# A batch's last half block computed in the fourth block's tile, with full-size products, k casts on GpSimd and later expert work

## The chip, the cores and the metric

The kernel runs on one core of a Trainium2 chip. The metric is the device time of one execution in microseconds (us); lower is better. The core has five engines that run their own instruction queues side by side: TensorE (PE, matrix products; PEld is its loading of weights), VectorE (DVE), ScalarE (ACT), GpSimd (POOL) and SyncE (SP, which here only issues DMAs). They meet through semaphores.

## The reference

Two stages, the output of the first being the input of the second.

Attention: q, k and v of 8 batches, 8 heads, 576 positions, 64 columns. A position sees itself and the 127 before it (`rel >= 0` and `rel < 128`), with a bias of minus slope times distance, one slope a head. Softmax, then the product with v. This gives x, 4608 tokens by 512 columns.

Mixture of experts: `logits = x @ w_gate` (8 experts), an exponential, eight rounds of dividing rows and columns by their sums (Sinkhorn), and then

```
for e in range(E):
    h = np.maximum(x @ w1[e], 0.0)
    ye = h @ w2[e]
    out += P[:, e:e + 1] * ye
```

with 1024 hidden columns an expert. So all eight experts run on all tokens.

## The kernel before

**The two halves of the span.** Until about 279 us the attention runs, with experts 0 and 1 of blocks that are ready as filler on PE. Then comes Sinkhorn, with the rest of that filler, and from about 332 us the experts 2 to 7, mostly in a seven-product (Strassen) form. The change touches the first half.

**Blocks and steps.** A batch of 576 positions is four blocks of 128 (kb = 0 to 3) and a last half block of 64 (kb = 4, `TL` = 64). The main loop (line 693) runs over steps (b, kb, u), u being one half of the heads; `at = 2 * kb + u` counts the ten steps of a batch. A step first prepares the next one: `scores` (key block kb against query blocks kb and kb + 1, PE, lines 407 to 428), `exps` (ACT, line 434), `masks` (DVE, a product with a table of the decayed and masked weights, line 447). Between them the filler issues expert matmuls. Then `values` of the present step (PE, line 472): queries of block kb against keys of block kb - 1 and kb; the 65th column of v is one, so the sum of the weights comes along. DVE divides (lines 482 and 483), and `turn_x` brings the result into the transposed form for the experts: by PE in batches 0 to 2 and 7, by a transposing DMA on SP in batches 3 to 6.

**The half block.** Its queries and keys lie in a tile of their own, tT: queries in columns 0 to 63, keys in columns 64 to 127. The scores of kb = 3 are 192 wide (128 own queries and 64 of the half block), those of kb = 4 are 64 by 64 with 64 keys. The values of kb = 4 use 64 columns of weights: four products with 128 keys and four with 64.

**How q and k get there.** `load_qk(b + 2)` is issued in batch b at step 3 (SP, line 275). `cast_qk` brings them to half precision, q on DVE and k on ACT, in four parts: from batch 4 on, two parts at steps 8 and 9 of batch b and two at steps 0 and 1 of batch b + 1. Then `turn_qk` transposes them by DMA (SP, line 305) and `order_qk` puts the rows in order: k on GpSimd right away, q on DVE at steps 6 and 7 (line 316). The scores of the next batch are issued in step 9. Batches 0 to 2 use PE transposes instead (`turn_pe`).

**The order of the work.** Each engine executes its instructions in the order in which the program issues them; nothing is reordered. A cast that waits for a load therefore holds all that was issued behind it on the same engine.

**The filler.** `Filler` holds units of expert work (blocks of tokens, expert 0 or 1). `filler.ready` says up to which block x exists. In each step the backlog is divided by `left`, the number of steps it is to be spread over (line 696), and that much is issued. For batches over `XPE` = 3 a batch's blocks become ready after step 0 of the next one (line 742).

**GpSimd** casts v five blocks ahead (`cast_v`, lines 388 and 389, with a memset of the column of ones), casts some parts of q and the half blocks, and issues the loads of the experts' weights.

**Constant matmuls.** `spin` and `spin_alone` issue matmuls on a constant tile (line 253) whose result nobody reads.

Of the kernel before, what the change touches and what calls it, by code (L numbers as in the profile page):

```python
# [14 lines left out]
def kernel(  # L15
# [10 lines left out]
    nc = tc.nc  # L26
# [206 lines left out]
    if True:  # L233
        mask = asb.tile([P, H, 2 * P], FP16, name="mask")
        rel = per.tile([P, HD], FP16, name="rel", tag="yo", bufs=YO)[:, 0 : 2 * P]

        def make_mask(ys):
            for y in ys:
                nc.scalar.activation(
                    out=mask[:, y, :], in_=rel, func=AF.Exp, scale=-float(slopes[head_of[y]])  # L240
                )

# [78 lines left out]
        def turn_tail(b):  # L321
            t16 = asb.tile([P, HD], FP16, name=f"t16_{b}", tag="xsb", bufs=XSB)
            nc.gpsimd.tensor_copy(out=t16, in_=tails.pop(b).rearrange("p h d -> p (h d)"))
            nc.sync.dma_start(out=QKT[b][2], in_=t16, transpose=True)
# [21 lines left out]
        def turn_pe(b, kq, j):  # L346
# [16 lines left out]
            if wide:  # L363
                nc.scalar.copy(out=QKT[b][2], in_=ps)
                return
# [18 lines left out]
        def cast_v(m):  # L384
# [4 lines left out]
            nc.gpsimd.memset(vt[:, :, Dh : Dh + 2], 1.0)  # L389
# [8 lines left out]
        def sizes(kb):  # L398
            nk = P if kb < NKB - 1 else TL
            nn = 0 if kb == NKB - 1 else (P if kb < NKB - 2 else TL)  # L400
            return nk, nn
# [5 lines left out]
        def scores(b, kb, u):  # L407

            nk, nn = sizes(kb)
            ps = sps.tile([P, 2, 2, 2 * P], FP32, name=f"psS_{b}_{kb}_{u}", tag="psS", bufs=2)  # L410
            both = kb < NKB - 2
            for y in range(2):
                j = 2 * u + y
                for hb in range(2):
                    n = 2 * P if both else nk
                    nc.tensor.matmul(  # L416
                        out=ps[0:nk, hb, y, 0:n],
                        lhsT=cols(b, 1, j, hb, kb),
                        rhs=cols(b, 0, j, hb, kb, 1 + both),
                    )  # L420
                for hb in range(2):
                    if nn and not both:
                        nc.tensor.matmul(
                            out=ps[0:nk, hb, y, nk : nk + nn],
                            lhsT=cols(b, 1, j, hb, kb),
                            rhs=cols(b, 0, j, hb, kb + 1),
                        )
            pss[b, kb, u] = ps

        def exps(b, kb, u):  # L430
            nk, nn = sizes(kb)
            ps = pss.pop((b, kb, u))
            pt = asb.tile([P, 4, 2 * P], FP16, name=f"pt_{b}_{kb}_{u}", tag="pt", bufs=4)
            nc.scalar.activation(  # L434
                out=pt[0:nk, :, 0 : nk + nn],
                in_=ps[0:nk, :, :, 0 : nk + nn].rearrange("p a y n -> p (a y) n"),
                func=AF.Exp,
                scale=scale,
            )
            pts[b, kb, u] = pt  # L440

        def masks(b, kb, u):
            nk, nn = sizes(kb)
            pt = pts[b, kb, u]
            hs = slice(4 * u, 4 * u + 4)
            w = nk + nn
# [802 lines left out]
```

## Time and profile before

| | us |
|---|---|
| median of three runs | 1013.42 |
| lowest and highest run | 1010.76, 1014.03 |
| the profiled execution | 1012.89 |
| its span, first to last instruction | 1011.1 |
| PE busy | 998.0 |
| DVE busy | 758.4 |
| ACT busy | 727.4 |
| POOL busy | 79.2 |

A row of instructions in order of time has its start, its length, engine, line, operation, output and inputs by the program's names, and in brackets the idle time before it with what ended it. `128*64` behind a matmul is the size of its weights (rows by columns), the shape after it that of the output. Lengths of neighbouring PE instructions overlap, so what a group costs is read from its start to the start of the next. In a row of a group, the busy time and the mean of one instruction stand behind the bar. `SPq` is the issue of a DMA; when it lands is not in that row.

### The profile page before, as it was taken

To read this page: it belongs to the slowest core of one execution; us is meant where nothing else is said; L and a number is where in the kernel's file an instruction comes from. 1 tells how busy PE (TensorE), PEld (TensorE's weight loads), DVE (VectorE), ACT (ScalarE), POOL (GpSimd) and SP (SyncE) were. 2 spreads that over 40 slices of the span, in tenths; PEclk is the share of its full clock that TensorE was granted. 3 is DMA by queue.
4 is the path that set the end of the run, shared out by engine and by line. 5 is a ranking of instruction groups with operands and counts; after the bars stand their busy time and mean duration, and the time that the engine had idled before them with its cause. 6 is when DMAs were issued, how large, how long until landed. Compare 5 with 4: busy or idle time off the path is not lost.

```text
span 1011.1 us, 27987 instructions
## 1 busy us (share of the span) xinstructions
PE 998.0 (99%) x11583; PEld 802.8 (79%) x11583; DVE 758.4 (75%) x1614; ACT 727.4 (72%) x1252; POOL 79.2 (8%) x143
## 2 busy tenths in 40 slices
PE   8999999999999999999999999999999999999998
PEld 5645444444544799999999999999999999999997
DVE  5737666655578989877877887887887787787787
ACT  7655554555333668888888888888888888888885
POOL 2312033315110000000000000000000000000000
PEclk9999999999999999999999999999999999999999
DMA  9997689888999334334333324335433333433361
GB/s 239 232 268 190 153 224 227 190 191 162 225 192 195 75 64 98 77 65 96 74 65 95 74 65 97 80 62 99 82 66 88 86 80 69 96 75 69 96 116 48
DMA packets 264431, 122.46 MB, mean 121 GB/s; under 512 B 201968, under 2 KB 255728, under 8 KB 264304
## 3 DMA queue, kind: packets, MB, share of 16 engines
q1 hardware_dynamic: 249568, 102.68, 44.8%
q0 software_dynamic: 14304, 17.84, 10.5%
q8 instruction: 90, 1.47, 0.6%
q14 instruction: 37, 0.30, 0.1%
q10 hardware_dynamic: 432, 0.16, 0.1%
HBM read 78.30 MB, written 23.59 MB: 101 GB/s over the span
## 4 chain that ended last, share of the span: by engine, by line
PE 92%; DVE 3%; DMA 2%; ACT 1%; issue 0%; SPq 0%; POOL 0%; DVEq 0%; ACTq 0%; POOLq 0%
PE psM L1020 31%; PE psB L983 14%; PE psh L117 12%; PE psy L141 11%; PE psA L983 9%; PE psC L983 9%; PE psN L472 2%; DMA k<-in_k_dram 2%; PE psS L416 2%; ACT pt L434 1%; PE psT L355 1%; PE psX L510 0%; DMA qk<-c 0%; DVE pt L447 0%; PE psh L962 0%
## 5 line engine op out<-in xcount | busy, mean ns | idle before, releaser
L1020 PEld LDWEIGHTS <-hs 128*128 128x128 f16 x2996 | 270.9, 98 | 22.6 <-DVE hs L1000 0.4
L1020 PE MATMUL psM<-w2l,hs 128*128 128x256 f16 x1440 | 186.7, 273 | 0.2 <-DVE hs L1000 0.2
L983 PEld LDWEIGHTS <-w1l 128*128 128x128 f16 x2848 | 181.3, 98 | 4.9 <-issue 0.5
L996 ACT ACTIVATE hs<-hs 128x512 f16<-128x512 f16 x212 | 130.2, 629 | 35.4 <-DVE hs L1166 25.8
L983 PEld LDWEIGHTS <-s 128*128 128x128 f16 x2136 | 141.6, 98 | 6.5
L1166 DVE TENSOR_TENSOR hs<-psB,s5y 128x512 f16<-128x512 f32 x106 | 73.3, 691 | 97.6 <-ACT xs L892 89.4
L117 PE MATMUL psh<-xT,w1t 128*128 128x512 f16 (+1 forms) x608 | 140.1, 372 | 0.4 <-ACT hT L129 0.4
L892 ACT ACTIVATE xs<-xtok,L_sb 128x512 f16<-128x512 f16 x204 | 136.3, 721 | 3.8 <-DMA xset<-xs 3.6
L129 ACT ACTIVATE hT<-psh 128x512 f16<-128x512 f32 (+1 forms) x144 | 83.3, 586 | 75.9 <-PE psh L117 75.8
L141 PE MATMUL psy<-w2t,hT 128*128 128x512 f16 x576 | 135.5, 380 | 0.0
L1020 PE MATMUL psM<-more,hs 128*128 128x256 f16 x864 | 129.5, 273 | 0.0
L983 PE MATMUL psB<-xset,s 128*128 128x128 f16 x1424 | 108.7, 219 | 0.0
L983 PE MATMUL psA<-xset,w1l 128*128 128x128 f16 x1424 | 108.6, 219 | 0.0
L141 PEld LDWEIGHTS <-hT 128*128 128x128 f16 x576 | 53.4, 98 | 59.6 <-issue 1.9
L434 ACT ACTIVATE pt<-psS 128x1024 f16<-128x1024 f32 (+2 forms) x80 | 67.6, 851 | 43.7 <-PE psS L416 20.3
L117 PEld LDWEIGHTS <-w1t 128*128 128x128 f16 x608 | 55.1, 99 | 53.3 <-issue 4.3
L559 DVE CAST yo<-psy 128x512 f16<-128x512 f32 x65 | 44.7, 691 | 61.6 <-PE psy L141 59.1
L1000 DVE TENSOR_TENSOR hs<-hs 128x1024 f16<-128x1024 f16 x107 | 73.9, 690 | 20.9 <-ACT hs L996 18.8
L1157 ACT COPY psC<-psB 128x512 f32<-128x512 f32 x106 | 60.4, 570 | 39.1 <-PE psB L983 39.1
L1149 ACT COPY s5y<-psC 128x512 f32<-128x512 f32 x106 | 62.1, 586 | 21.6 <-PE psC L983 21.5
L447 DVE TENSOR_TENSOR pt<-pt,mask 128x1024 f16<-128x1024 f16 (+2 forms) x80 | 52.4, 656 | 33.5 <-ACT pt L434 33.4
L1064 DVE TENSOR_TENSOR acc<-acc,psM 128x256 f32<-128x256 f32 (+1 forms) x162 | 73.9, 502 | 0.3
(122 smaller groups left out, 1400.1 us busy)
## 6 DMA issues: line engine op xcount, KB each, us to landing
s5y<-ysp SPq DMA_DIRECT2D x36, 256.0 KB, 3.0
ysp<-yo SPq DMA_DIRECT2D x65, 128.0 KB, 3.5
v<-in_v_dram SPq DMA_DIRECT2D x32, 256.0 KB, 4.2
out_dram<-acc SPq DMA_DIRECT2D x31, 256.0 KB, 2.5
q<-in_q_dram SPq DMA_DIRECT2D x5, 1024.0 KB, 7.7
k<-in_k_dram SPq DMA_DIRECT2D x5, 1024.0 KB, 9.4
xtok<-xd SPq DMA_DIRECT2D x34, 128.0 KB, 2.2
w2t<-in_moe_w_dram POOLq DMA_DIRECT2D x4, 1024.0 KB, 12.6
```

Source lines behind the costliest of these rows:

```text
L117: nc.tensor.matmul(out=ps[:, 0:nt], lhsT=w1ts[e][:, dt, P * ft : P * ft + P], rhs=xT[:, at : at + nb, dt, :], start=(dt == 0), stop=(dt == ...
L129: nc.scalar.activation(out=st["hT"][:, ft, 0:nt], in_=ps[:, 0:nt], func=AF.Relu)
L141: nc.tensor.matmul(out=ps, lhsT=st["hT"][:, ft, P * ms : P * ms + P], rhs=w2ts[e][:, ft, :], start=(ft == 0), stop=(ft == NFT - 1),)
L434: nc.scalar.activation(out=pt[0:nk, :, 0 : nk + nn], in_=ps[0:nk, :, :, 0 : nk + nn].rearrange("p a y n -> p (a y) n"), func=AF.Exp, scale ...
L892: nc.scalar.mul(out=xs[2 * (n % 2) + m], in_=xtok[m], mul=P_sb[:, blk, e : e + 1])
L983: nc.tensor.matmul(out=ps[:, j, :], lhsT=q[k][:, P * j : P * j + P], rhs=xset[n % 2][:, x, P * k : P * k + P], start=(start and j == 0 and ...
L996: nc.scalar.activation(out=h[n][:, slot], in_=src, func=AF.Relu)
L1000: nc.vector.tensor_tensor(out=t[:, 4:6], in0=t[:, 0:2], in1=t[:, 2:4], op=ALU.add)
L1020: nc.tensor.matmul(out=Ms[bk][:, half, :], lhsT=h[n][:, LEFT[m], f, :], rhs=W2L[e][RIGHT[m]][:, f, :], start=(e == 2 and f == 0 and half = ...
L1064: nc.vector.tensor_tensor(out=a, in0=a, in1=p2, op=op)
L1149: nc.scalar.copy(out=s5, in_=pc)
L1166: nc.vector.tensor_tensor(out=h[n][:, 3], in0=pb, in1=s5, op=ALU.add)
```

## The change

1. `scores` of kb = 4 are dropped as a step. The tile of kb = 3 becomes 256 wide: columns 0 to 63 are the half block's keys against its queries, 64 to 127 the fourth block's keys against the half block's queries, 128 to 255 the fourth block against itself. tT gets 64 zero columns, so that the half block's 64 keys are loaded as 128 columns of weights.
2. `exps` and `masks` of kb = 4 go; those of kb = 3 work on 1024 columns instead of 768. The mask table is 3 x 128 wide, its first part made on GpSimd in `tail_masks`.
3. `values` always uses 128 columns of weights and 128 rows; for the half block the lower 64 rows of v are set to zero, its ones included.
4. k's cast is on GpSimd from batch 3 on.
5. The filler's units of a batch become ready after step 1 of the next batch, and `left` is moved by one step (and by one for batch 3).
6. Eight constant matmuls stand ahead of the values of step (1, 1, 0).
7. At the start, two v casts, two q casts and the load of expert 0's w2 stand later in the program, behind `tail_masks`.

```diff
-        mask = asb.tile([P, H, 2 * P], FP16, name="mask")
+        mask = asb.tile([P, H, 3 * P], FP16, name="mask")
+        mask_of = {kb: mask[:, :, P : 3 * P] if kb < NKB - 2 else mask[:, :, 0 : 2 * P] for kb in range(NKB - 1)}
...
+        def tail_masks():
+
+            nc.gpsimd.memset(mask[TL:P, :, 0:TL], 0.0)
+            nc.gpsimd.tensor_copy(out=mask[0:TL, :, 0:TL], in_=mask[0:TL, :, P : P + TL])
+            nc.gpsimd.tensor_copy(out=mask[:, :, TL:P], in_=mask[:, :, 2 * P : 2 * P + TL])
...
-            TT = asb.tile([P, NDT, P], FP16, name=f"tT_{b}", tag="tT", bufs=2)
+            TT = asb.tile([P, NDT, P + TL], FP16, name=f"tT_{b}", tag="tT", bufs=2)
+            nc.gpsimd.memset(TT[:, :, P : P + TL], 0.0)
...
-            nc.gpsimd.memset(vt[:, :, Dh : Dh + 2], 1.0)
+            if nk < P:
+                nc.gpsimd.memset(vt[nk:P], 0.0)
+            nc.gpsimd.memset(vt[0:nk, :, Dh : Dh + 2], 1.0)
...
             for y in range(2):
                 j = 2 * u + y
-                for hb in range(2):
-                    n = 2 * P if both else nk
-                    nc.tensor.matmul(
-                        out=ps[0:nk, hb, y, 0:n],
-                        lhsT=cols(b, 1, j, hb, kb),
-                        rhs=cols(b, 0, j, hb, kb, 1 + both),
-                    )
-                for hb in range(2):
-                    if nn and not both:
-                        nc.tensor.matmul(
-                            out=ps[0:nk, hb, y, nk : nk + nn],
-                            lhsT=cols(b, 1, j, hb, kb),
-                            rhs=cols(b, 0, j, hb, kb + 1),
-                        )
+                if kb < NKB - 2:
+                    parts = [(0, 2 * P, [cols(b, 1, j, hb, kb) for hb in range(2)], [cols(b, 0, j, hb, kb, 2) for hb in range(2)])]
+                else:
+                    tail_q = [cols(b, 0, j, hb, NKB - 1) for hb in range(2)]
+                    tail_k = [QKT[b][2][64 * hb : 64 * hb + 64, j, TL : TL + P] for hb in range(2)]
+                    own_k = [cols(b, 1, j, hb, kb) for hb in range(2)]
+                    parts = [
+                        (P, P, own_k, [cols(b, 0, j, hb, kb) for hb in range(2)]),
+                        (TL, TL, own_k, tail_q),
+                        (0, TL, tail_k, tail_q),
+                    ]
+                for at, n, ks, qs in parts:
+                    for hb in range(2):
+                        nc.tensor.matmul(out=ps[:, hb, y, at : at + n], lhsT=ks[hb], rhs=qs[hb])
...
-                        ops.append((hh, pts[b, kb - 1, u][:, 2 * hb + y, P : P + nk], vs[b, kb - 1][:, 4 * u + hh, 0 : Dh + 1]))
-                    ops.append((hh, pts[b, kb, u][0:nk, 2 * hb + y, 0:nk], vs[b, kb][0:nk, 4 * u + hh, 0 : Dh + 1]))
-            if kb == NKB - 1:
-                ops = ops[0::2] + ops[1::2]
+                        t, at = (pts[b, kb - 1, u], P) if kb < NKB - 1 else (pts[b, kb - 1, u], TL)
+                        ops.append((hh, t[:, 2 * hb + y, at : at + P], vs[b, kb - 1][:, 4 * u + hh, 0 : Dh + 1]))
+                    t, at = (pts[b, kb, u], P * (kb == NKB - 2)) if kb < NKB - 1 else (pts[b, kb - 1, u], 0)
+                    ops.append((hh, t[:, 2 * hb + y, at : at + P], vs[b, kb][:, 4 * u + hh, 0 : Dh + 1]))
...
-        cast_v(3)
-        cast_v(4)
-        for j in (2, 3):
-            cast_qk(1, j, (0,), True)
-        load_weights(0, 1, 2)
...
             turn_pe(0, 1, j)
             turn_pe(0, 0, j)
+        tail_masks()
+        cast_v(3)
+        cast_v(4)
+        for j in (2, 3):
+            cast_qk(1, j, (0,), True)
+        load_weights(0, 1, 2)
...
-            left = ((10 - at) % 10 + 1) if b >= XPE else 10 - at + 9 * (at == 9)
-            budget = filler.backlog() / (11 if (b, at) == (XPE, 0) else left)
+            left = (11 - at) % 10 + 1 if b > XPE else 12 - at if b == XPE else 10 - at + 9 * (at == 9)
+            budget = filler.backlog() / left
...
-                elif nxt[2] == 0:
+                elif nxt[2] == 0 and nxt[1] < NKB - 1:
                     scores(*nxt)
                     scores(*nxt[:2], 1)
-                exps(*nxt)
+                if nxt[1] < NKB - 1:
+                    exps(*nxt)
             got = filler.fill(1.0) if b else 0.0
-            if nxt:
+            if nxt and nxt[1] < NKB - 1:
                 masks(*nxt)
+            if (b, kb, u) == (1, 1, 0):
+                spin_alone(8)
             values(b, kb, u)
...
-            if at == 0 and b > XPE:
+            if at == 1 and b > XPE:
                 filler.ready = 4 * b
...
             if XPE <= b + 1 < B - 1 and at >= 8:
-                cast_qk(b + 2, at - 8)
+                cast_qk(b + 2, at - 8, (1,), True)
+                cast_qk(b + 2, at - 8, (0,))
             if XPE <= b + 1 < B:
                 if at == 0 and b + 1 == XPE:
-                    cast_qk(b + 1, 0)
-                    cast_qk(b + 1, 1)
+                    for j in range(2):
+                        cast_qk(b + 1, j, (1,), True)
+                        cast_qk(b + 1, j, (0,))
                 if at < 2:
-                    cast_qk(b + 1, at + 2)
+                    cast_qk(b + 1, at + 2, (1,), True)
+                    cast_qk(b + 1, at + 2, (0,))
```

More of the change, by code (lines that the diff above doesn't have):

```diff
@@ L239, in make_mask @@
                 nc.scalar.activation(
-                    out=mask[:, y, :], in_=rel, func=AF.Exp, scale=-float(slopes[head_of[y]])
+                    out=mask[:, y, P : 3 * P], in_=rel, func=AF.Exp, scale=-float(slopes[head_of[y]])
                 )
+        def tail_masks():
+            nc.gpsimd.memset(mask[TL:P, :, 0:TL], 0.0)
+            nc.gpsimd.tensor_copy(out=mask[0:TL, :, 0:TL], in_=mask[0:TL, :, P : P + TL])
+            nc.gpsimd.tensor_copy(out=mask[:, :, TL:P], in_=mask[:, :, 2 * P : 2 * P + TL])
         raw: dict = {}
@@ L440, in exps @@
             pts[b, kb, u] = pt
         def masks(b, kb, u):
-            nk, nn = sizes(kb)
             pt = pts[b, kb, u]
-            hs = slice(4 * u, 4 * u + 4)
-            w = nk + nn
-            nc.vector.tensor_tensor(
-                out=pt[0:nk, :, 0:w], in0=pt[0:nk, :, 0:w], in1=mask[0:nk, hs, 0:w], op=ALU.mult
-            )
+            nc.vector.tensor_tensor(out=pt, in0=pt, in1=mask_of[kb][:, 4 * u : 4 * u + 4, :], op=ALU.mult)
         xsbs: dict = {}
         def values(b, kb, u):
-            nk, _ = sizes(kb)
+            nk = sizes(kb)
```

22 lines of the change are left out of this document (6 added, 16 removed).

## The prediction

> **What bounds the kernel now.** I read the page's busy times first, then the list of waits of PE, then the busy times by stage around the one dip of the clock, and last the instructions in order of time there and in one undisturbed batch. Page, part 1, then the one row of PE's waits that is over 1.1 us in total, then four stages (columns: stretch, its length, busy us and count of PE, weight loads, DVE, ACT, POOL, granted clock, DMA share, GB/s):
>
> ```profile
> PE 998.0 (99%) x11583; PEld 802.8 (79%) x11583; DVE 758.4 (75%) x1614; ACT 727.4 (72%) x1252; POOL 79.2 (8%) x143
> ```
> ```profile
> PE psN L472 <- DVE pt L447: 4.6, 6, 1.7
> ```
> ```profile
> 25.00:50.00 25.00, 23.44 (x285) 16.91 (x283) 19.34 (x49) 16.36 (x29) 7.66 (x17) 1.00 1.11 233
> 139.80:141.50 1.70, 0.01 (x1) 0.00 (x0) 0.71 (x2) 1.70 (x4) 0.13 (x1) 1.00 1.25 271
> 141.50:144.00 2.50, 2.38 (x19) 1.10 (x20) 2.43 (x7) 2.12 (x3) 0.53 (x2) 0.80 0.51 134
> 144.00:147.80 3.80, 3.80 (x17) 1.55 (x16) 1.91 (x6) 1.83 (x4) 0.66 (x2) 0.68 0.58 168
> ```
>
> PE is busy 99% of the span, so time can be gained in two ways only: fewer or quicker matmuls, and fewer waits of PE. PE's waits on the mask product (L447) are 4.6 us in all, one of them 1.7. That one lies at 139.8 us, where PE stands still for 1.70 us, and behind it the granted clock is 0.80 for 2.5 us and 0.68 for 3.8 us: 0.20 x 2.5 + 0.32 x 3.8 = 1.7 us more are lost to the clock. The first row is for comparison: 1.56 us idle in several pieces, clock 1.00.
>
> Who holds PE at 139.8, in order of time on PE, ACT, DVE and SP:
>
> ```profile
> 135.05 0.61 PE L416 MATMUL psS<-qN,kN 64*128 64x256 f16 x8
> ...
> 137.91 1.90 PE L141 MATMUL psy<-w2t,hT 128*128 128x512 f16 x8
> 141.54 0.30 PE L472 MATMUL psN<-v,pt 128*128 128x65 f16 x4 [1.73 <-DVE pt L447]
> ```
> ```profile
> 139.22 0.62 ACT L293 CAST c<-k 128x512 f16<-128x512 f32 x1 [7.39 <-DMA k<-in_k_dram]
> 139.74 1.02 ACT L434 ACTIVATE pt<-psS 128x1024 f16<-128x1024 f32 x1
> ```
> ```profile
> 133.55 1.14 DVE L316 COPY qN<-qk 128x512 f16<-128x512 f16 x2
> ...
> 136.28 0.43 DVE L291 CAST c<-q 128x512 f16<-128x512 f32 x1
> ...
> 140.79 0.69 DVE L447 TENSOR_TENSOR pt<-pt,mask 128x1024 f16<-128x1024 f16 x1 [2.57 <-ACT pt L434]
> ```
> ```profile
> 128.54 2.28 SPq L275 DMA_DIRECT2D q<-in_q_dram  x1
> 130.87 0.58 SPq L275 DMA_DIRECT2D k<-in_k_dram  x1
> ```
>
> The scores were ready at about 135.6, but ACT sat 7.39 us in front of a k cast whose load was issued only at 130.87. The exponential stood behind that cast in ACT's queue, the mask product behind the exponential, and PE behind the mask product. This is the step from batch 3 to batch 4; the cast is of batch 5.
>
> **The change part by part.** *The values of a last half block* (`values`, kb = 4) are 8 matmuls per step, 4 with 128x64 and 4 with 64x64 weights; the change makes all 8 full 128x128, at the same 65 columns. One undisturbed batch on PE:
>
> ```profile
> 192.18 0.19 PE L423 MATMUL psS<-tT,kN 64*128 64x64 f16 x2
> 192.20 0.22 PE L416 MATMUL psS<-qN,kN 64*128 64x128 f16 x2
> ...
> 194.53 1.89 PE L141 MATMUL psy<-w2t,hT 128*128 128x512 f16 x8
> 196.26 1.03 PE L117 MATMUL psh<-xT,w1t 128*128 128x512 f16 x4
> 197.12 0.41 PE L472 MATMUL psN<-v,pt 128*128 128x65 f16 x8
> 197.37 1.89 PE L117 MATMUL psh<-xT,w1t 128*128 128x512 f16 x8
> 199.19 0.31 PE L416 MATMUL psS<-tT 64*64 64x64 f16 x8
> 199.43 1.04 PE L117 MATMUL psh<-xT,w1t 128*128 128x512 f16 x4
> ...
> 202.28 1.89 PE L141 MATMUL psy<-w2t,hT 128*128 128x512 f16 x8
> 204.09 0.56 PE L472 MATMUL psN<-v,pt 128*64 128x65 f16 x8
> 204.58 1.90 PE L141 MATMUL psy<-w2t,hT 128*128 128x512 f16 x8
> ```
>
> Durations overlap, so I read from start to next start. Eight wide expert matmuls take 196.26 - 194.53 = 1.73 us. Eight full-size values take 197.37 - 197.12 = 0.25. The half-size ones could have begun at 202.28 + 1.73 = 204.01 and the next work begins at 204.58: 0.57. So each step gains 0.32 us, and there are 2 x 8 of them: 5.1 us. Ends: 0, if half the size is not what made them slow, and 5.1.
>
> *The scores of a last half block* go from an own block of 8 (64x64) into the tile of kb = 3, where they are 8 more of 64x128 beside 16. Removed: from 197.37 + 1.73 = 199.10 to 199.43, 0.33 us a batch. Added: four pairs of 64 columns; such a pair takes 0.02 to 0.03 us (192.18 to 192.20), so 0.1, or 0.25 if they run like the removed block's own 8 (199.19 to 199.43). I take 0.13, nearest to the pair that stands in the same tile, and gain 0.20 x 8 = 1.6 us; ends 0.6 and 1.8.
>
> *The exponentials and masks of kb = 4* (16 each on ACT and DVE) go; those of kb = 3 widen from 768 to 1024 columns. No PE wait stands at these steps in a filled batch, so this is 0 on the path; the cover is the expert work between. In batch 0 nothing covers: the wider exponential and mask come some 0.4 us later (1.02 us for 1024 columns, so 0.25 for a quarter, and a quarter of 0.69), and the scores of kb = 4 are no longer in the way (0.3). Nothing.
>
> *The zeroed halves.* Each batch gets a memset of tT's 64 new columns and of v's lower 64 rows, and the start gets three instructions for the third mask part, all on GpSimd; `cast_v(3)`, `cast_v(4)`, two q casts and the load of w2t stand behind the three. Batch 0's last half block is the tight place:
>
> ```profile
> 23.19 0.60 POOL L388 CAST v<-v 64x512 f16<-64x512 f32 x1 [1.55 <-DMA v<-in_v_dram]
> ```
> ```profile
> 24.07 0.56 PE L472 MATMUL psN<-v,pt 128*64 128x65 f16 x8
> 24.56 0.44 PE L510 MATMUL psX<-ident,xsb 128*128 128x128 f16 x4
> 24.84 0.82 PE L253 MATMUL psJ<-ones 128*128 128x256 f16 x6
> 25.49 3.66 PE L117 MATMUL psh<-xT,w1t 128*128 128x256 f16 x32
> ```
>
> The cast ends at 23.8; the zeroing comes behind it (at most as long as the cast, 0.6), so the values there start between 24.1 and 24.4 instead of at 24.07 and take 0.25 less. 0, ends -0.4 and +0.3. The mask part itself is prepared while GpSimd waits for that v anyway.
>
> *Eight constant matmuls* ahead of the values of (1, 1, 0). Six take 25.49 - 24.84 = 0.65, so eight take 0.87. PE waits there already:
>
> ```profile
> 38.05 0.32 PE L472 MATMUL psN<-v,pt 128*128 128x65 f16 x5
> 39.33 0.39 PE L472 MATMUL psN<-v,pt 128*128 128x65 f16 x7 [0.96 <-DVE pt L447]
> ```
>
> They lie inside the 0.96 us. 0; if that wait were gone, -0.87.
>
> *k casts to GpSimd* (20 casts, batches 3 to 7). ACT is freed, and with it the exponential at 139.74: the mask product is no longer behind the k load. Late next is the q load, which holds DVE: `c<-q` stands before a `yo` cast and this mask product in DVE's queue. It ran at 136.28 with no wait to speak of, so q was there by then; 136.28 + 0.43 + 0.69 + 0.69 = 138.1 at the latest, without the half-width starts overlapping 137.4. PE wants it at 139.8 before; after, the expert work of batch 3 is spread over 12 steps instead of 11, and by the issue order eight expert matmuls fewer (1.73 us) lie between batch 3's first values and this point, with 0.84 us less from the two parts above (2 x 0.32 + 0.20): 137.2. Remaining wait 0.2 to 0.9, I take 0.4: gain 1.3 of 1.7. The clock stays up after a wait of that size (0.96 us above left 1.00): gain 1.7. Ends for both: 0 and 3.4.
>
> Behind a waiting k cast on GpSimd stand the v casts, the zeroing and, at the end, the kN copies; SP's transposes of c wait for the last k cast. In an undisturbed batch:
>
> ```profile
> 182.29 0.61 POOL L388 CAST v<-v 128x512 f16<-128x512 f32 x1 [4.95 <-DMA v<-in_v_dram]
> ...
> 193.21 4.45 POOL L316 COPY kN<-qk 128x512 f16<-128x512 f16 x4 [10.26 <-DMA qk<-c]
> ```
> ```profile
> 185.44 5.48 SPq L305 DMA_TRANSPOSE qk<-c  x2
> ```
>
> The last k cast comes right behind the v cast, 182.9 to 183.5 (up to 184.1 under contention), and SP gets to the transposes at 185.44: 1.3 us spare. kN ends at 197.7, its scores start at 206.41. So nothing in batches 4 to 6. At 135.05 there is less: DVE ended the qN copies at 134.7, 0.35 ahead of the scores, and those come 2 us sooner relative to SP's work while the copies move along with DVE's queue. I charge 0.3 there, ends 0 and 1.
>
> *The filler's half-block delay* moves the same matmuls; PE is packed from 142 us on, so it changes no sum: 0. It moves a few stores on SP behind the x transposes; their landing is waited for by nobody within 4 us.
>
> Sum: 5.1 + 1.6 + 1.3 + 1.7 - 0.3 = 9.4 us. From the profiled execution's 1012.89 (the median of the three runs is 0.5 above it): **1003.5 us**.
>
> **Rivals.** (a) *The wait stays, turned to q or kN*: the stop of 1.7 us and its clock loss come back at the same boundary. For it: q lands within 1 us of being needed. Against: k lands 3 us after q. 9.4 - 3.0 = 6.4 us: 1006.5.
>
> (b) *The clock dips anyway.* The wait of 1.70 us is followed by 0.80 and 0.68, other waits up to 0.96 by 1.00; that the one caused the other is inferred from one case. If not, 1.7 us stay lost: 1005.2. The Trainium skill, "TensorE: Matmul & The Clock Gate", section "Part 1: The HAM clock gate", has the clock halve after a window of about 3.4 us without work, which would speak for this rival, as PE's stop is half as long; the trace shows the dip behind the shorter stop.
>
> (c) *The size is not the cause*: the half blocks cost 0.57 for another reason, such as their own masks arriving. Against: no wait is listed there, and the scores pay 0.09 at their start as well. 1003.5 + 5.1 = 1008.6.
>
> (d) *Slower: GpSimd becomes late.* If the last k cast slips by more than the 1.3 us and the 8.7 us behind it, each boundary of batches 3 to 7 stops PE like the one at 139.8, 1.7 + 1.7 us. From three boundaries on (10.2 against 9.4) it is slower; with all five, 1003.5 + 17 = 1020.5. For it: the kN copies take 1.1 us each and slow DVE beside them:
>
> ```profile
> 193.34 1.36 DVE L447 TENSOR_TENSOR pt<-pt,mask 128x768 f16<-128x768 f16 x1 [0.43 <-ACT pt L434]
> ```
>
> 768 columns in 1.36 us, where 1024 took 0.69 alone. Against, one filled batch by the busy times of its stage:
>
> ```profile
> 171.00:205.00 34.00, 34.00 (x266) 16.59 (x265) 21.90 (x49) 18.55 (x30) 9.95 (x15) 1.00 0.92 204
> ```
>
> GpSimd is busy 9.95 of 34 us and gets four casts of 0.6 and the zeroing, some 3 to 4 us. The Trainium skill, "SBUF — State Buffer", section "SBUF: two separate sides", has GpSimd and a DVE product with two SBUF inputs take one pair of ports in turns, each for a whole instruction: by it 20 casts hold DVE 12 us at most in all. The row of the 768 columns agrees in kind, and DVE is busy 21.90 of 34 us there.
>
> **Chances.** Forecast 0.63; (a) 0.12; (b) 0.09; (c) 0.06; (d) 0.07, of which a little ends even; 0.03 for an unseen gain at the start. A difference under 0.3% (3 us) can't be told from none. Faster 0.89 (forecast, a, b, c but for its edge), same 0.04, slower 0.07. The forecast's own range is 1001 to 1005.5; to hold 8 in 10 it takes in (a), (b) and most of (c): 1000.0 to 1009.0.
>
> **What would show it.** The values of kb = 4 as 128x128 groups of eight at 0.25; the scores of kb = 3 as one block of 24 in about 0.6; no ACT cast of k after batch 2 and no wait over 1 us of PE near 137 us, clock 1.00 there; GpSimd's k casts at 0.6 to 1.1 and the transposes of c no later behind them. It is wrong if a PE wait of more than 1 us stands at a batch boundary, or if PE's total of idle grows at the start by more than the half microsecond allowed.

## The result and the profile after

The changed kernel takes 1007.44 us (median of 11 runs, 1006.52 to 1012.48) against 1011.86 us of the kernel before (11 runs, 1009.68 to 1014.03). The ratio is 0.9955, with a 95% interval from 0.9944 to 0.9967: 4.4 us faster, where 9.4 were forecast. The profiled execution took 1010.98 us, with a span of 1009.2; its mean granted clock was 0.998, and runs with 0.998 or less are 2 of 11 of the changed kernel (median 1010.8 against 1006.9 for the rest) and 42 of 85 of the kernel before beside the experiments (1013.7 against 1011.4).

The page's busy times and the first rows of PE's list of waits (total us, how often, longest) of the changed kernel:

```profile
PE 992.1 (98%) x11591; PEld 802.0 (79%) x11591; DVE 760.0 (75%) x1598; ACT 717.9 (71%) x1216; POOL 102.5 (10%) x182
```
```profile
PE psN L467 <- DVE pt L444: 2.9, 5, 1.2
PE psh L117 <- DMA xT<-xsb: 2.8, 2, 2.3
PE psT L363 <- ACT c L300: 2.0, 3, 1.0
PE psN L467 <- DVE xsb L478: 1.6, 2, 1.3
```

PE's work fell by 5.9 us (998.0 to 992.1), the span by 1.9 only. The wait of 1.7 us on the mask product is gone; in its place stands a wait that the kernel before didn't have, for the transposed x (xT), 2.3 us long. The half block's products in one undisturbed batch, in order of time on PE:

```profile
184.73 0.23 PE L433 MATMUL psS<-qN,kN 64*128 64x128 f16 x2
...
185.29 1.90 PE L141 MATMUL psy<-w2t,hT 128*128 128x512 f16 x8
...
200.95 0.41 PE L467 MATMUL psN<-v,pt 128*128 128x65 f16 x8
201.19 3.62 PE L141 MATMUL psy<-w2t,hT 128*128 128x512 f16 x16
```

Twenty-four score products take 185.29 - 184.73 = 0.56 us, and eight values of the half block 201.19 - 200.95 = 0.24: both as forecast. Now the two boundaries where the time went. First from batch 3 to 4, on PE:

```profile
137.10 0.29 PE L467 MATMUL psN<-v,pt 128*128 128x65 f16 x4
...
140.39 1.02 PE L117 MATMUL psh<-xT,w1t 128*128 128x512 f16 x4 [0.50 <-DMA xT<-xsb]
```

The values that stood still until 141.54 start at 137.10, without a stop; 1.7 of the 4.4 us between are expert work that the delay has moved behind this point. Three microseconds later PE waits for x instead, 0.50 us here. From batch 6 to 7 it waits longer. PE, SP's issues, GpSimd, and two stages of the busy times (columns as in the prediction; the figure behind the five engines is the granted clock):

```profile
240.57 0.29 PE L467 MATMUL psN<-v,pt 128*128 128x65 f16 x4
243.18 1.89 PE L117 MATMUL psh<-xT,w1t 128*128 128x512 f16 x4 [2.32 <-DMA xT<-xsb]
```
```profile
228.40 0.59 SPq L386 DMA_DIRECT2D v<-in_v_dram  x1
232.72 1.23 SPq L332 DMA_TRANSPOSE tT<-t  x1
...
234.66 1.44 SPq L518 DMA_TRANSPOSE xT<-xsb  x1
```
```profile
225.33 4.87 POOL L324 COPY kN<-qk 128x512 f16<-128x512 f16 x4 [10.29 <-DMA qk<-c]
...
232.08 0.61 POOL L331 CAST t<-t 128x512 f16<-128x512 f32 x1
```
```profile
243.20:246.00 2.80, 2.80 (x17) 1.58 (x18) 0.43 (x3) 0.60 (x1) 1.83 (x4) 0.50 1.05 322
246.00:249.00 3.00, 3.00 (x19) 1.21 (x18) 0.52 (x2) 1.54 (x3) 3.00 (x7) 0.92 0.85 133
```

SP has nothing to issue from 228.99 to 232.72: the next in its queue is the transpose of the half block (tT), which waits for GpSimd's cast of it (t), and that cast stands behind four kN copies and two v casts. The transpose of x of batch 6's fourth block, next but one behind it, is issued at 234.66 and lands about 8.5 us later, the longest landing of the twenty. PE stands for 2.32 us, and the clock is 0.50 for 2.8 us and 0.92 for 3.0: 1.40 + 0.24 = 1.6 us more.

The late issue is one half of this stop, the long landing the other. The same transpose in the kernel before, with the two loads of expert 2's weights (w2l, 256 KB each) that GpSimd issues near it; then these two loads in the changed kernel:

```profile
235.35 1.22 SPq L523 DMA_TRANSPOSE xT<-xsb  x1
236.83 1.41 POOL L594 DMA_DIRECT2D w2l<-in_moe_w_dram  x2
```
```profile
233.93 1.41 POOL L589 DMA_DIRECT2D w2l<-in_moe_w_dram  x2
```

Before, the transpose landed 5.3 us after its issue. Over the 14 traces of this case the landing goes with the order: where the first of the two loads was issued ahead of the transpose or at most 0.24 us behind it, the transpose took 6.9 to 10.1 us (seven traces); where the load came 0.69 us or more behind, 4.3 to 6.0 us (the other seven). With 6.0 us x would have been there at 240.6, just before PE asks for it at 240.86; issued without SP's pause of 3.73 us, it would have been there even with 8.5. So it takes both. That the loads lengthen the landing is not shown by a run that moves them alone.

### The profile page after: what moved, and what is told of

It is laid out like the page before. It is cut to its first block, busy times and chain, and to the rows that moved or that the text cites. A ratio compares the mean times of both kernels' runs of the same rounds, so it can differ in the third digit from the quotient of the medians.

```text
span 1009.2 us, 27982 instructions
## 1 busy us (share of the span) xinstructions
PE 992.1 (98%) x11591; PEld 802.0 (79%) x11591; DVE 760.0 (75%) x1598; ACT 717.9 (71%) x1216; POOL 102.5 (10%) x182
## 4 chain that ended last, share of the span: by engine, by line
PE 81%; DVE 3%; DMA 2%; ACT 0%; issue 0%; SPq 0%; DVEq 0%
PE psM L1022 31%; PE psB L985 14%; PE psA L985 9%; PE psC L985 9%; PE psh L117 8%; PE psy L141 7%; DMA xT<-xsb 2%; PE psN L467 1%; PE psS L433 1%; PE psh L964 0%; DMA s5y<-ysp 0%; DVE acc L1066 0%; DVE hs L1168 0%; DVE yo L554 0%; DVE acc L1042 0%
## 5 line engine op out<-in xcount | busy, mean ns | idle before, releaser
L439 ACT ACTIVATE pt<-psS 128x1024 f16<-128x1024 f32 x64 | 64.1, 1022 | 43.4 <-PE psS L433 35.5
L1147 ACT COPY psB<-psA 128x512 f32<-128x512 f32 x106 | 60.8, 573 | 18.4 <-PE psA L985 18.4
```

The costliest lines, as they stand in the source:

```text
L439: nc.scalar.activation(out=pt, in_=ps.rearrange("p a y n -> p (a y) n"), func=AF.Exp, scale=scale)
```

## The experiments

Theory A: the products and the k casts gave what the prediction's spacings say, and other waits took part of it back: the x transposes on SP, late behind the half block's cast and transpose. Rival B: the products gave little, because the half size was not what made them slow. Further rivals (the filler's new order, GpSimd's work, the DMA engines) stand in the expectations. All ratios are to runs of the kernel before in the same series (medians 1013.0, 1012.54 and 1012.45), with 95% intervals.

### The half block and the full products alone

```diff
...
+            left = ((10 - at) % 10 + 1) if b >= XPE else 10 - at + 9 * (at == 9)
+            budget = filler.backlog() / (11 if (b, at) == (XPE, 0) else left)
...
-            if (b, kb, u) == (1, 1, 0):
-                spin_alone(8)
...
+            if at == 0 and b > XPE:
...
-                cast_qk(b + 2, at - 8, (1,), True)
-                cast_qk(b + 2, at - 8, (0,))
+                cast_qk(b + 2, at - 8)
```

(against the changed kernel; the other k casts go back to ACT in the same way)

> The half block in the fourth block's tile with full-size products alone: k casts on ACT, the filler's order and the constant matmuls as before. Theory A (the products gave what their spacing says, and new waits behind GpSimd and SP gave it back): the values of kb = 4 at 0.25 us for eight, 5 to 7 us less than before, so 1005 to 1007 against 1011.9. Theory B (the full-size products gave little, the whole gain came from the k casts): within 2 us of before, 1010 to 1012. Under both the wait of about 1.7 us near 138 us behind the k cast on ACT stays.

Measured: 1008.46 us, ratio 0.9961 (0.9946 to 0.9975), 4 to 5 us faster than before, a little less than the 5 to 7 of theory A. Three rows on PE: the old stop, and the first rows of the gating products of batches 5 and 6 in this kernel, then in the kernel before:

```profile
139.86 0.30 PE L467 MATMUL psN<-v,pt 128*128 128x65 f16 x4 [2.72 <-DVE pt L444]
...
218.63 0.54 PE L526 MATMUL psG<-wg_sb,xT 128*128 128x8 f16 x16
251.75 0.54 PE L526 MATMUL psG<-wg_sb,xT 128*128 128x8 f16 x16
```
```profile
221.69 0.55 PE L531 MATMUL psG<-wg_sb,xT 128*128 128x8 f16 x16
255.74 0.55 PE L531 MATMUL psG<-wg_sb,xT 128*128 128x8 f16 x16
```

A filled batch takes 33.12 us instead of 34.05: 0.93 less, where 0.84 (two groups of values and a block of scores) was forecast. The old stop stays and grows from 1.73 to 2.72, since PE comes to it 2.7 us sooner and the mask product only 1.7. That is A in kind, and B falls.

### The k casts alone

```diff
-                cast_qk(b + 2, at - 8)
+                cast_qk(b + 2, at - 8, (1,), True)
+                cast_qk(b + 2, at - 8, (0,))
```

(on the kernel before; the other k casts likewise)

> Only the k casts go to GpSimd, all else as before. Theory A: the wait of PE behind the k load (1.7 us, and up to 1.7 us of clock behind it) goes or shrinks to under 1 us, 1 to 3.5 us less: 1008.5 to 1011. Theory B: 4 us less, 1008. If the casts on GpSimd hold DVE and PE by themselves: no gain or a loss, 1012 and more.

Measured: 1010.13 us, ratio 0.9974 (0.9963 to 0.9986). The stop on the mask product is gone from the list, and this is the next thing on PE:

```profile
140.60 1.02 PE L117 MATMUL psh<-xT,w1t 128*128 128x512 f16 x4 [0.86 <-DMA xT<-xsb]
```

So the x transpose stands right behind the k load: take the one stop away and the other is there, 0.86 us long. The two parts gain some 4 and 2.6 us alone (1 - 0.9961 and 1 - 0.9974 of 1012), 6.6 together, and the changed kernel has 4.5.

### The filler's order, with k on GpSimd and on ACT

First the changed kernel with the filler's order put back as before; then the changed kernel with only k's casts back on ACT, so that filler delay and constant matmuls stay.

```diff
-            left = (11 - at) % 10 + 1 if b > XPE else 12 - at if b == XPE else 10 - at + 9 * (at == 9)
-            budget = filler.backlog() / left
+            left = ((10 - at) % 10 + 1) if b >= XPE else 10 - at + 9 * (at == 9)
+            budget = filler.backlog() / (11 if (b, at) == (XPE, 0) else left)
...
-            if at == 1 and b > XPE:
+            if at == 0 and b > XPE:
```

> The changed kernel with the expert work of a batch ready after step 0 and spread as before. Theory A has the wait of PE on the transposed x (2.3 us and a clock dip of about 1.5 us, 0.5 us at an earlier boundary) as a matter of when x is asked for: asked for half a block earlier it grows, 1009 to 1012. Theory B, or if the delay of the expert work is worth nothing: 1007.4 as changed.

Measured: 1007.6 us (6 runs), ratio 0.995 (0.993 to 0.997), the same as the changed kernel, so the 1009 to 1012 of theory A did not come. Its waits did: those on x are longer without the delay.

```profile
PE psh L117 <- DMA xT<-xsb: 4.9, 3, 3.1
```

(Its profiled execution also stands 2.5 us at the start for a late v.)

```diff
-                cast_qk(b + 2, at - 8, (1,), True)
-                cast_qk(b + 2, at - 8, (0,))
+                cast_qk(b + 2, at - 8)
```

> The changed kernel with the k casts on ACT again. Theory A: the wait behind the k load comes back (1 to 3.5 us), what GpSimd's casts cost goes (up to 2 us): 1007 to 1009.5. Theory B: the gain is gone, 1011 to 1012.

Measured: 1012.18 us, ratio 1.000 (0.9985 to 1.0015). This is the number of rival B, but not its cause: with the shapes alone, k on ACT as well, it was 0.9961; the delay and the eight constant matmuls, which are all that differs, cost 3.7 us here. The stop on the mask product is 3.25 us, and in each later batch a small one on the mask product stands at its third step (0.37 to 0.41).

So the delay is not free. It keeps PE from asking for x too early and leaves less expert work to cover the masks at the start of a batch (that it is the delay and not the constant matmuls rests on these places, and on the next run, where the constant matmuls make no difference); with k on GpSimd the two come out even.

### Without the constant matmuls

```diff
-            if (b, kb, u) == (1, 1, 0):
-                spin_alone(8)
```

> The changed kernel without the eight constant matmuls ahead of the values of step (1, 1, 0). If they lie inside a wait that is there anyway (0 in the prediction's sum), the time stays at 1007.4 within 0.5 us, and the step's wait of PE on the mask product is longer by up to 0.9 us. If they cost time, the time falls by up to 0.9 us, to 1006.5. If they keep the clock up, the time rises by 1 to 2 us, with a granted clock under 1.00 in the stretch from 25 to 50 us.

Measured: 1008.2 us, ratio 0.9953 (0.9937 to 0.9968), beside 0.9955: no difference. The wait that covers them comes back at its old length:

```profile
39.95 0.39 PE L467 MATMUL psN<-v,pt 128*128 128x65 f16 x7 [0.96 <-DVE pt L444]
```

### The half block's cast on ACT

```diff
-            nc.gpsimd.tensor_copy(out=t16, in_=tails.pop(b).rearrange("p h d -> p (h d)"))
+            nc.scalar.copy(out=t16, in_=tails.pop(b).rearrange("p h d -> p (h d)"))
```

> The changed kernel with the half block's cast of q and k (t) on ACT in place of GpSimd, so that SP's transpose of it doesn't wait behind the kN copies. Theory A (the new waits of PE on the x transposes come from SP standing behind that transpose): the 2.8 us of waits on xT go to under 0.5, the clock dip after 243 us with them, and the time falls by 2 to 4 us, to 1003.5 to 1005.5. Rival B (the x transposes land late because the DMA queues are full, wherever they are issued): the waits stay and the time stays at 1007.4 within 0.7. Rival C (ACT's exponentials are tight, and 0.6 us more on ACT per batch turns up as waits on the mask product): xT waits go, waits on the mask product rise by as much, 1006.5 to 1008.

Measured: 1011.1 us, ratio 0.9984 (0.997 to 0.9998): by the ratios 3 us slower than the changed kernel. The waits on x are gone, as A said (the transpose of batch 6 is issued at 231.93 here, ahead of the two weight loads, and lands 6.0 us later), but none of the theories had what came in their place (C, the nearest, had it on the mask product and as work, not as a wait). ACT:

```profile
158.53 0.62 ACT L331 CAST t<-t 128x512 f16<-128x512 f32 x1 [5.49 <-DMA t<-in_k_dram]
```

The load of t is itself late, and ACT now stands in front of it for 3 to 5.5 us, once in each of three batches, with the hidden activations and exponentials queued behind; PE then waits 2.7 us in all for the hidden activations. It is the stop of the kernel before with another load. On GpSimd the same wait costs ACT nothing.

### The values with 64 columns of weights again

```diff
-                        ops.append((hh, t[:, 2 * hb + y, at : at + P], vs[b, kb - 1][:, 4 * u + hh, 0 : Dh + 1]))
+                        ops.append((hh, t[:, 2 * hb + y, at : at + nk], vs[b, kb - 1][:, 4 * u + hh, 0 : Dh + 1]))
...
-                    out=psN[:, hh, :],
+                    out=psN[0:nk, hh, :],
```

(the second operand's columns likewise)

> The changed kernel with the values of kb = 4 as products with 64 columns of weights again (the queries' columns cut to 64, the keys' rows stay 128), nothing else. Theory A (size alone makes them slow, 0.57 against 0.25 us for eight): 16 groups x 0.32 = 5.1 us more, 1012.5. Rival B (size is not the cause): 1007.4 within 0.7, and the groups take 0.25. Rival C (only groups in which 64 and 128 rows of weights alternate pay, and columns alone do not): a tenth of a microsecond a group, 1009.

Measured: 1010.3 us, ratio 0.9975 (0.9962 to 0.9989): 2 us more than the changed kernel by the ratios, 2.9 by the medians. On PE, and the groups of weight loads by shape (busy us, mean ns):

```profile
133.69 1.90 PE L141 MATMUL psy<-w2t,hT 128*128 128x512 f16 x8
135.52 0.44 PE L467 MATMUL psN<-v,pt 128*64 128x65 f16 x8
135.89 0.82 PE L141 MATMUL psy<-w2t,hT 128*128 128x512 f16 x3
```
```profile
L467 PEld LDWEIGHTS <-pt 128*128 128x128 f16 x448 | 21.9, 98 | 19.3 <-DVE pt L444 7.5
L467 PEld LDWEIGHTS <-pt 128*64 128x64 f16 x128 | 5.3, 110 | 7.0 <-issue 5.1 <-DVE xsb L478 1.1 <-DVE rden L477 0.4
```

Eight products with 64 columns take 135.89 - 133.69 - 1.73 = 0.47 us, against 0.24 with 128 columns and 0.57 in the kernel before, where four products with 128 rows were followed by four with 64. So of the forecast 0.32 a group 0.23 go with the columns and 0.10 with the rows; 16 x 0.23 = 3.7 us, against 2 to 3 measured. Loading half the weights is not quicker: 110 ns for 64 columns, 98 for 128. The Trainium skill, "TensorE: Matmul & The Clock Gate", section "LDWEIGHTS (loading the stationary operand)", gives a time in proportion to the columns, which by estimate would make it 53 ns; the measurement differs. The next section of that page, "Weight-path perf modes — Fast Weight Load (FWL) and DoubleRow", asks for the full 128 columns for the fast load, and with that the two rows agree in kind.

### Both gains together, without delay and with the half block's cast on ACT

The lines of the filler and the constant matmuls as in the first experiment, the half block's cast as in the experiment of that name; k's casts stay on GpSimd.

```diff
+            if at == 0 and b > XPE:
...
+            nc.scalar.copy(out=t16, in_=tails.pop(b).rearrange("p h d -> p (h d)"))
```

> The changed kernel with three parts of it set differently: the filler's order as before, no eight constant matmuls, and the half block's cast on ACT. What stays of the change is the half block in the fourth tile, the full-size products and the k casts on GpSimd. Theory A (the x transposes on SP are what took back the gain of the k casts): both gains add, 4.5 us of the shapes and 2.9 us of the k casts, 1004.5, with no wait on xT over 0.5 us and none on the mask product over 1 us after 100 us. Rival B (the gains overlap for another reason, such as the DMA share at the batch boundary): 1007.5 as with the filler order alone.

Measured: 1007.98 us, ratio 0.9951 (0.9932 to 0.9969), the same as the changed kernel. One stop is left after 100 us, and the clock behind it is 0.50; the third row is the first product after the attention:

```profile
140.28 1.86 PE L117 MATMUL psh<-xT,w1t 128*128 128x512 f16 x4 [2.48 <-DMA xT<-xsb]
...
326.09 0.61 PE L983 MATMUL psA<-xset,w1l 128*128 128x128 f16 x8
```
```profile
140.20:143.00 2.80, 2.72 (x10) 1.06 (x10) 1.31 (x4) 0.60 (x1) 0.44 (x2) 0.50 0.66 198
```

At 326.09 this execution is 5.8 us ahead of the kernel before (331.88, the row stands below). With the stop of 2.48 and its clock loss of 1.4 away it would be 9.7, near the prediction's sum of 9.4. Here the half block's cast no longer holds SP, and x is late all the same. Behind the loads of q and k (125.60 to 127.84) three of SP's next six issues take 2.1 to 3.1 us instead of 0.6 to 1.2, two of these three shown here; PE waits for the transpose in the last row:

```profile
130.06 3.06 SPq L518 DMA_TRANSPOSE xT<-xsb  x1
...
134.49 2.63 SPq L332 DMA_TRANSPOSE tT<-t  x1
...
137.85 1.19 SPq L518 DMA_TRANSPOSE xT<-xsb  x1
```

### The loads of q and k one step earlier

Four kernels have this edit. The first is the kernel just described with it, the second that with the half block's cast back on GpSimd, the third the changed kernel with it, the fourth the kernel before with it.

```diff
-            if 1 <= b < B - 2 and at == 3:
+            if 1 <= b < B - 2 and at == (2 if b >= XPE else 3):
                 load_qk(b + 2)
```

> The run before this one (the changed kernel with the filler's order as before, no constant matmuls and the half block's cast on ACT) with one edit: batches 3 to 5 issue their loads of q and k one step earlier on SP, at step 2 in place of step 3, so ahead of an x transpose instead of behind it. Theory A (the loads of q and k, 1 MB each, fill SP's queue, each issue behind them takes 2 to 3 us, and so the x transpose of a batch's fourth block comes too late for PE at 140 us): the transpose of that block is issued 1 to 3 us sooner, the 2.5 us wait shrinks to under 1 us, the clock stays at 1.00 there, and the time falls by 1 to 3 us, to 1005 to 1007. Rival B (the DMA engines are full in that stretch, whatever the order of issue): wait and time as without the edit, 1008.

Measured: 1006.73 us (6 runs), ratio 0.994 (0.9922 to 0.9959); within the 1005 to 1007 of theory A, but not separable from 0.9951 or from the changed kernel. The stop shrinks to 1.39 and the clock stays at 1.00 behind it:

```profile
142.36 1.04 PE L117 MATMUL psh<-xT,w1t 128*128 128x512 f16 x4 [1.39 <-DMA xT<-xsb]
```

This execution is 3.0 us later from the start on, because of a late v; counted from the gating products of batch 2 in each (121.89 here, 118.91 without the edit) the transpose is issued 0.9 us sooner (139.94 and 137.85), and the stop is 1.1 us shorter. That is theory A in kind, a little below its lower end (1 us sooner, a stop under 1 us).

> As the first run of this call, with the half block's cast on GpSimd as in the changed kernel. If SP's transpose of the half block waits behind GpSimd's kN copies, the waits on xT are longer than with the cast on ACT, by up to 2 us in all, and the time is 0.5 to 2 us longer. If the place of that cast doesn't matter with this order of the filler, both take the same time within 0.5 us.

Measured: 1012.5 us, ratio 1.0002 (0.9985 to 1.002). The one difference between these two kernels is the engine of the half block's cast, and it is worth 5.8 us, where 0.5 to 2 were expected. PE, GpSimd and SP:

```profile
144.19 1.89 PE L117 MATMUL psh<-xT,w1t 128*128 128x512 f16 x4 [4.44 <-DMA xT<-xsb]
```
```profile
137.86 1.05 POOL L396 CAST v<-v 128x512 f16<-128x512 f32 x1 [5.39 <-DMA v<-in_v_dram]
...
138.90 0.89 POOL L331 CAST t<-t 128x512 f16<-128x512 f32 x1
```
```profile
136.81 0.59 SPq L386 DMA_DIRECT2D v<-in_v_dram  x1
139.82 1.23 SPq L332 DMA_TRANSPOSE tT<-t  x1
...
141.77 1.19 SPq L518 DMA_TRANSPOSE xT<-xsb  x1
```

The chain is whole here, over three queues: a load of v that now stands behind 2 MB of q and k; GpSimd waiting 5.39 us for it, with the half block's cast behind; SP with nothing to issue from 137.40 to 139.82, with the x transpose behind; PE waiting 4.44 us.

> The changed kernel with the loads of q and k of batches 3 to 5 issued one step earlier, nothing else. Theory A: the small wait on xT at 140 us (0.5 us) goes, but the casts of the half block on GpSimd stay where they are, so the wait near 240 us can come back; 0 to 1.5 us faster than the changed kernel, 1006 to 1007.4. Rival B: 1007.4.

Measured: 1014.46 us, ratio 1.0015 (1.0001 to 1.003), by the ratios some 6 us slower than the changed kernel where 0 to 1.5 faster was expected. Its cast is on GpSimd. The profiled execution, one of the shorter with 1011.8 us, has four waits on x, the longest 1.34 and 1.87 us, and several on the hidden activations of up to 0.69; between 100 and 330 us its waits are 7.3 us in all, against 5.0 in the changed kernel, at a clock of 1.00. What the other runs lose beyond that is open; a lowered clock, 0.998 or less in eight of the 12, is part of it.

> The kernel before with the loads of q and k of batches 3 to 5 issued one step earlier, k's cast left on ACT. If PE's stop of 1.7 us at the boundary from batch 3 to 4 comes from the late issue of the k load, it shrinks by about the 2 to 3 us that the load comes sooner: under 0.5 us, clock 1.00, and 1.5 to 3 us faster than before, like the k casts on GpSimd by themselves (2.9). If the load is late because the DMA engines are busy, the wait stays and the time is the same.

Measured: 1016.37 us, ratio 1.0036 (1.002 to 1.0053): slower too, where 1.5 to 3 us faster was expected. The stop on the mask product is gone, so the k load was late by its place in SP's queue, and 4.00 us on x stand in its place; the cast is the one that waits:

```profile
140.29 0.97 POOL L388 CAST v<-v 128x512 f16<-128x512 f32 x1 [6.31 <-DMA v<-in_v_dram]
```

## Why the prediction was right, and where it was off

Faster was right, and 1007.4 lies within the range; the time was 3.9 us too low, and of the 9.4 us forecast 4.4 came. The range held because it was drawn wide enough for three rivals. And the prediction's own sign of being wrong came true: a wait of PE of more than 1 us at a batch boundary (2.32 us).

*The values of kb = 4* (5.1 us): right in mechanism and size. Eight take 0.24 against 0.57, and the size is the cause: with 64 columns 0.23 us a group and 2 to 3 us in all come back, and the rest goes with the 64 rows. Rival (c) falls.

*The scores* (1.6 us): 0.56 us for 24 against 0.45 for the 16 before (192.11 to 192.56) and 0.33 for the block of their own: 0.22 a batch, forecast 0.20.

*Batches 0 and 1* were counted at the full 0.84 each and gave 0.3 together (0.0 to 0.9 in four other traces with the same start). The gating products of batch 1, before and after, and the first product after the attention, before and after:

```profile
87.74 0.55 PE L531 MATMUL psG<-wg_sb,xT 128*128 128x8 f16 x16
...
331.88 0.61 PE L983 MATMUL psA<-xset,w1l 128*128 128x128 f16 x8
```
```profile
87.41 0.54 PE L526 MATMUL psG<-wg_sb,xT 128*128 128x8 f16 x16
...
329.97 0.61 PE L985 MATMUL psA<-xset,w1l 128*128 128x128 f16 x8
```

At the start PE's waits on ACT's casts for the transposes (0.8 us before, 2.0 after) and ahead of the half block (0.77 before, 1.33 after) take it. "Nothing covers" was said of batch 0, and still the gain of its products was booked.

*The exponentials and masks of kb = 4* (0): the cover named there, the expert work between, is what the delay takes away. In the changed kernel PE waits 1.16 us for the wider mask product in batch 3 (at 125.92), and in no kernel without the delay does it wait there.

*The constant matmuls* (0): right.

*The k casts* (1.3 us of wait): the stop at 139.8 is gone altogether, no mask wait is left there, and neither q nor kN takes its place, so rival (a) as it was put falls. But its kind was right: a stop does come back, and it is x. The step that failed is the sentence on what is late next, "Late next is the q load, which holds DVE". The q load was not next; the x transpose of batch 3's fourth block was: PE waits 0.86 us for it in the kernel before with the k casts alone. DVE's queue was followed and SP's wasn't.

*The clock* (1.7 us): there was no dip behind the boundary from batch 3 to 4, as forecast, but the kernel before has a lowered clock in about half of its runs only (42 of 85), so on a median this term is worth about half; and in the profiled execution it came back with the stop at 243 us. Rival (b) is half right: what dips is tied to a stop, and there was another.

*The filler's half-block delay* (0): the step with its reason was wrong in both halves. "It moves a few stores on SP behind the x transposes; their landing is waited for by nobody within 4 us" priced the stores, not the transposes, whose landing PE waits for. And "PE is packed from 142 us on, so it changes no sum" overlooked that the moved work was cover: with k on ACT, delay and constant matmuls cost 3.7 us; with k on GpSimd the small waits it adds and the waits on x it saves come out even. In place of 0, the small waits are some 2.5 us (the account below).

*GpSimd* (0, 1.3 us spare for the transposes of c): the k casts themselves did no harm, and (d) in its own form, a slower kernel through late transposes of c, did not occur. But GpSimd is late in another place, at the half block's cast, and SP is behind that. The prediction had looked at one of the two things that SP waits for from GpSimd.

The account of the profiled execution, up to the first product after the attention: 331.88 - 329.97 = 1.9 us gained of 9.4. Missing 7.5: the stop on x at 243 us, 2.3; its clock loss, 1.6; batches 0 and 1, 1.68 - 0.33 = 1.35; the other waits of PE between 100 and 330 us, 2.5 (1.16, 0.50, 0.42 and two of about 0.2) against 0.4 before, 2.1. That makes 7.35. But the stop that went, 1.73, had been booked with 1.3 - 0.3 = 1.0 only, so some 0.9 us have no cause here.

Without the stop at 243 us and its clock loss the gain would be 5.8. One trace shows such an execution: that of the changed kernel without the constant matmuls, whose program is the same from 40 us on. PE at the boundary from batch 6 to 7, and its first product after the attention:

```profile
240.18 1.02 PE L117 MATMUL psh<-xT,w1t 128*128 128x512 f16 x4
...
326.41 0.61 PE L983 MATMUL psA<-xset,w1l 128*128 128x128 f16 x8
```

It has no wait on x and a clock of 1.00 from 120 to 260 us, and gains 331.88 - 326.41 = 5.5 us. Nine of the eleven runs of the changed kernel have a median 4.0 us below the profiled one, as runs without the stop and the clock loss (2.3 + 1.6) would; that they are such runs is inferred. So the new stop explains the profiled execution, and not the usual one, in which 3.9 of the 9.4 us are missing as well. In this trace 1.6 are missing in batches 0 and 1, and 2.5 in other waits between 100 and 330 us (3.0 against 0.5 before), each under 0.8 us, four of six on the mask product. Kernels without the delay have at most 0.3 us of waits on the mask product or v there, apart from the stop behind the k load. With the 0.7 that the old stop gave over its booking, 3.4 of the 3.9 are found.

With the filler's order as before, k and the half block's cast off each other's engine, and its one stop on x taken out in arithmetic, the sum is 9.7. So the terms of the products and of the removed stop were right. Three others were not: the stop that takes the place of the one removed was missed, the delay was put at 0, and the gain at the start was booked in full.

What stays open: how x can be had in time at both boundaries in every run; in the trace just shown it is, in that of the changed kernel it isn't. The shortest median, that of the earlier loads with the cast on ACT, is 1006.73 us, which can't be told from the changed kernel. Another place for the x transpose ahead of the half block's in SP's queue wasn't tried, nor a later place for the weight loads alone.

## What to carry to other kernels

When an edit removes a stop, list what each queue would deliver next at that place, SP's included, and subtract: here PE waited 0.86 us for x as soon as the k cast was out of the way, and the stop moved rather than went. An edit that only moves work is not worth nothing by that: ask what the work covered where it stood. A cast that stands on an engine between a late load and a DMA ties three queues together; before a cast is moved, look at what stands behind it on the new engine, and who issues behind its result. And gains per product count where PE is packed; a start that waits for its loads doesn't pay them.

## What the runs showed of the hardware

Weights of 64 columns load no quicker than of 128 (110 against 98 ns), and a group of eight small products with them takes 0.47 us against 0.24; with 64 rows in the second four of the group it is 0.57.

The clock falls behind some stops of PE and not behind others of nearly the same length: to 0.50 behind 2.32, 2.48 and 1.73 us, and not behind 1.39 us, nor behind 1.87 us in the changed kernel with the earlier loads:

```profile
245.26 1.04 PE L117 MATMUL psh<-xT,w1t 128*128 128x512 f16 x4 [1.87 <-DMA xT<-xsb]
```
```profile
245.20:248.00 2.80, 2.46 (x21) 1.39 (x22) 1.48 (x4) 0.60 (x1) 0.97 (x2) 1.00 1.10 266
```

When it falls, it is by one size. The 0.80 and 0.68 of the kernel before, read over one stretch, are 0.50 for 3.4 us, a loss of 1.7:

```profile
143.00:146.40 3.40, 3.40 (x13) 1.35 (x12) 2.88 (x8) 1.59 (x3) 0.66 (x2) 0.50 0.53 153
```

Added up over windows of 2 us from 20 to 340 us, the loss is 1.70 to 1.72 us in eight of the 14 traces, three times that, 5.12, in the earlier loads with the cast on GpSimd, and nothing in the other five.

The Trainium skill, "TensorE: Matmul & The Clock Gate", section "Part 1: The HAM clock gate", has the clock at half or full, decided in free-running windows of about 3.4 us. The 0.50, the 3.4 us and the chance in it agree, since a stop can fall within a window or across two; the table there has the clock fall after an idle window, and the stops of 1.73, 2.32 and 2.48 us are shorter than one.

Behind two issued loads of 1 MB, in the trace with both gains together, three of the next six issues of SP took 2.1 to 3.1 us, the others 0.6. A transpose of x took 2.3 to 8.5 us from issue to landing in the changed kernel, with a median of 3.4; near the boundary from batch 6 to 7 the long landings (6.9 to 10.1 us) are those with two loads of weights issued ahead of or with the transpose.
